# Attention, gated convolution and expert layer on one core: the first two batches in one written order of single steps, part of the low halves on GpSimd

## The chip, the core and the metric

The kernel runs on one core of a Trainium2 chip. The metric is device time in microseconds (us) of one execution. Engines are named as the profile names them: PE (TensorE matmul) with PEld (its weight load), DVE (VectorE), ACT (ScalarE), POOL (GpSimd) and SP (SyncE, which issues the DMAs).

## The reference

For each of 8 batches, 8 heads of width 64 and 576 positions, a linear attention, an RMS norm, a gated value layer with a 5-tap convolution, and a second, larger layer. The expert weights arrive as float64, which the device takes as pairs of 32-bit words.

```python
kv  = einsum('bhsd,bhse->bhde', k, v)                 # per head, 64 x 64
out = einsum('bhsd,bhde->bhse', q, kv)
x   = out / sqrt(mean(out*out, -1) + 1e-6) * g_norm   # heads side by side: 576 x 512
gate = sigmoid(sum_k conv_w[k] * x_padded[k:k+576])   # 5 taps along the positions
x   = (gate * (x @ w_val)) @ w_out                    # 512 x 512 each; "y" below
# then the second layer: w_in (512 x 1024), gelu, norm, w_sg over positions, w_out, residual
```

## The kernel before

A batch's 576 positions are five tiles of 128 (the last one overlaps and brings 64 new ones). Everything that a matmul reads is kept as a high part, rounded to the format that TensorE takes at full speed, and a low part, the difference to the full value; a product of two split operands is three matmuls per slice of 128 (`gemm3`, L228: high by high, low by high, high by low), 12 matmuls for one 128x512 tile.

One batch goes through these steps. `kv` (L280) multiplies K and V of all tiles, and ACT copies the eight 64x64 blocks into a block-diagonal tile `kvbd` (L288, L289). `o` (L296) multiplies q of one tile by it. ACT squares (L302), DVE sums over the head (`reduce`, L305), the mean is taken on DVE for batch 0 and on GpSimd for the others (L306), GpSimd raises it to -0.5 (`pow`, L307), and DVE multiplies the tile by it (`scale`, L310). PE turns the tile round (`xT`, L325), ACT writes its high part (`Xh`, L329) and its full value (`X`, L330), and DVE the low part from PSUM (`Xl`, L334). The convolution is one tap on ACT (L353) and four on DVE for each of four column groups (`taps`, L359), the sigmoid is ACT's (L362). `val` is the product with w_val (L228), DVE multiplies it by the gate (`gated`, L387), ACT makes its high part (L388), and DVE or GpSimd its low part (`z low`, L391; GpSimd for two of four from batch 1 on). `y` is the product with w_out, copied by ACT (L405) and stored (L407).

The two weights w_val and w_out are split on the chip in four pieces each. A piece is one ACT step (L131), TENSOR_SCALAR steps on DVE (L141, L142, L143), two SCALAR_TENSOR_TENSOR steps on DVE (L134, L138), a high part on ACT (L178), and then the low part. For all of w_val and the first piece of w_out, the low part is the sum of three PE matmuls (label `l`, L196) copied by ACT (L197); for the other pieces of w_out it is a subtraction (L186) and an addition (L188) on DVE.

The order is partly written out: all of batch 0 up to its `z low` parts stands under a manual schedule, in which each engine gets its instructions in program order. Then a loop over batches and eight steps per batch (four `val`, four `y`) puts one product of the current batch, one or two `o` tiles of the next, and the deferred work of earlier steps (a list with due slots, `later`) one behind the other. Every PE result takes one of eight PSUM banks (`bank`, L89), in order of request. `busy(n)` puts n matmuls without use on PE. After the last batch a second phase follows, with products hv, hu, sg and out on PE to the end.

Loads go through one queue on SP, in program order; a load whose buffer is not free holds up all behind it.

Of the kernel before, what the change touches and what calls it, by code (L numbers as in the profile page):

```python
# [13 lines left out]
I32 = mybir.dt.int32  # L14
# [51 lines left out]
def body(ctx, tc, qT, k, v, gcol, w_val, conv_w, w_out, w_in, g_ln, w_sgT, b_sg, w_out2, out, out_r):  # L66
# [45 lines left out]
    nc.gpsimd.memset(mhalf, -0.5)  # L112
    kvbd = [sb(f"kvbd{i}", [NK, P]) for i in range(2)]
# [31 lines left out]
    def split(src, h, l, raw=None, tmp=None, k=None, last=nc.gpsimd.tensor_tensor):  # L145
# [20 lines left out]
        def first():  # L166
            if wide:
                st["steps"] = wide_parts(st["raw"].rearrange("p (n t) -> p n t", t=2),
                                         sb("cv", [3, n]) if tmp is None else tmp)
                st["steps"][0]()  # L170

        def steps():

            ops = st["steps"][1]
            yield ops[0]()
            yield ops[1]()
            a = ops[2]()
            act(h, flat(a), AF.Copy)  # L178
            yield
            yield ops[3]()  # L180
            c = ops[4]() if last else ops[4](l, flat)
            yield
            if last is None:
                st["parts"] = a, c
                return
            last(flat(a), flat(a), f32(h), op=ALU.subtract)  # L186
            yield
            tt(l, flat(a), flat(c), op=ALU.add)  # L188
            yield

        def summed():

            a, c = st["parts"]
            ps = bank("l", n)
            for i, (w, x) in enumerate(((ident, flat(a)), (signed[:, 1], h), (signed[:, 0], c))):
                nc.tensor.matmul(flat(ps), lhsT=w, rhs=x, start=(i == 0), stop=(i == 2))  # L196
            return lambda: act(l, flat(ps), AF.Copy)  # L197

        def rest():
            r = st["raw"]  # L200
            if wide:
                for _ in steps():
                    pass
# [8 lines left out]
        return load, work, first, steps if wide else lambda: iter([rest()]), summed if wide and last is None else lambda: lambda: None  # L212
# [32 lines left out]

    class Attention:
        def __init__(self, b):
            self.b = b
            self.xh, self.xl = (sb(f"X{b % 2}{i}", [NK, MAIN], F32R) for i in "hl")

        def load_kv(self):
            b = self.b
            self.k, self.v = sb("K", [5, D]), sb("V", [5, D])
            for c in (((0, 2), (2, 4)) if b == 0 else ((0, 4),)):
                for t_, src in ((self.k, k), (self.v, v)):
                    dma(t_[:, c[0]:c[1], :], src[b, P * c[0]:P * c[1], :].rearrange("(c p) d -> p c d", p=P))
            dma(self.k[:, 4, :], k[b, TOK[4]:, :])
            dma(self.v[REST:, 4, :], v[b, MAIN:, :])
            nc.gpsimd.memset(self.v[:REST, 4, :], 0.0)

        def load_q(self):
            self.q = sb("Q", [NK, S])
            dma(self.q, qT[self.b].rearrange("m p s -> p m s"))

        def kv(self, half):
            if half == 0:
                if self.b:
                    pk = bank("kv")
# [13 lines left out]
            if half:  # L282
                later(0, self.kv_out, 0)

        def kv_out(self):
            bd = kvbd[self.b % 2]
            for pk, j in self.pk3:
                act(bd[:DH, j, :DH], pk[:DH, :, :DH], AF.Copy)  # L288
                act(bd[DH:, j, DH:], pk[DH:, :, DH:], AF.Copy)  # L289

        def o(self, t, wait=3):
            bd = kvbd[self.b % 2]
            o = TOK[t]
            po = bank("o")
            for j in range(NK):
                nc.tensor.matmul(po[:, j * P:(j + 1) * P], lhsT=self.q[:, j, o:o + P], rhs=bd[:, j, :], start=True, stop=True)  # L296
            st = sb("st", [3, 8], bufs=5)
            xo = tmp(D)
            x3 = xo.rearrange("p (h d) -> p h d", d=DH)

            def square():
                act(xo, po, AF.Square)  # L302

            def norm(small=nc.gpsimd.tensor_scalar):
                nc.vector.tensor_reduce(st[:, 0], x3, axis=AX.X, op=ALU.add)  # L305
                small(st[:, 1], st[:, 0], 1.0 / DH, 1e-6, op0=ALU.mult, op1=ALU.add)  # L306
                nc.gpsimd.tensor_tensor(st[:, 2], st[:, 1], mhalf, op=ALU.pow)  # L307

            def scale():
                tt(x3, po.rearrange("p (h d) -> p h d", d=DH),  # L310
                   st[:, 2].unsqueeze(2).to_broadcast([P, 8, DH]), op=ALU.mult)

            if wait is None:
                square()
                return norm, scale, lambda: self.transpose(t, xo, True)
            later(0, square, 0)
            later(0, norm, 0)
            later(wait - 1, scale, 0)
            later(wait, lambda: self.transpose(t, xo), 0)

        def transpose(self, t, xo, apart=False):
            o, n = (TOK[t], P) if t < 4 else (MAIN, REST)
            pt = bank("xT")
            for j in range(NK):
                nc.tensor.transpose(pt[:, j * P:(j + 1) * P], xo[:, j * P:(j + 1) * P], ident)  # L325
# [659 lines left out]
```

## Time and profile before

| | |
|---|---|
| time, median of 3 runs | 728.8 us (728.15 to 728.98) |
| profiled execution | 727.04 us |
| its span in the trace | 725.2 us, so 1.84 us lie around the span |
| PE busy | 709.9 us (98% of the span) |
| DVE, ACT, POOL busy | 583.6, 350.3, 152.5 us (80%, 48%, 21%) |
[...]
| y of batch 1 begins on PE | at 93.15 us |

Rows of the timeline hold the start, the duration, the engine, the line, the operation, the tile written and the tile read with their shapes, and the number of instructions in a run; square brackets give the idle time of that engine before the row and what ended it. Where a run has several instructions, its duration from the first start to the last end says less than the distance of their starts, which is what the prediction counts with ("pitch"): 7.38 us for ten taps is a pitch of 0.74.

### The profile page before, as it was taken

The numbers are of one execution on the slowest core, as the hardware profiler recorded it, in microseconds if no ns is written. First come the engines' busy times: TensorE is split into PE (matmuls) and PEld (weight loads), VectorE is DVE, ScalarE is ACT, GpSimd is POOL, SyncE is SP. The second block draws the span as 40 slices with busy tenths as digits, with TensorE's granted clock in tenths as the row PEclk, the third lists the DMA queues.
The fourth block names the chain that finished last, engine by engine and source line by source line (L and its number), as shares of the span: only waits on it lengthen the run. The fifth ranks groups of instructions, "written<-read, shape, count | busy, mean of one in ns | idle before, by whom it ended". The sixth has DMA issues, their size and how long they took to land.

```text
span 725.2 us, 11759 instructions
## 1 busy us (share of the span) xinstructions
PE 709.9 (98%) x4490; PEld 620.7 (86%) x4490; DVE 583.6 (80%) x1127; ACT 350.3 (48%) x667; POOL 152.5 (21%) x173
## 2 busy tenths in 40 slices
PE   8997999999999999999999999999999999999998
PEld 7785888879888888899889889898899898898897
DVE  6699979999989999699976866867856857867662
ACT  4667465676566674475433433424333424334230
POOL 1414437262727361112000000000100000100000
PEclk9999999999999999999999999999999999999999
DMA  9945253525462213433220321122241122111202
GB/s 338 331 141 201 96 195 119 217 80 207 130 251 84 88 30 125 158 120 103 73 81 36 103 89 30 58 88 74 78 156 30 58 88 74 58 59 45 102 1 87
DMA packets 56712, 81.19 MB, mean 112 GB/s; under 512 B 3665, under 2 KB 29265, under 8 KB 55633
## 3 DMA queue, kind: packets, MB, share of 16 engines
q1 hardware_dynamic: 56656, 80.45, 32.2%
q8 instruction: 35, 0.57, 0.3%
q14 instruction: 21, 0.16, 0.1%
HBM read 61.56 MB, written 18.87 MB: 111 GB/s over the span
## 4 chain that ended last, share of the span: by engine, by line
PE 58%; DVE 1%; DMA 0%; ACT 0%; POOL 0%; issue 0%; POOLq 0%; SPq 0%; DVEq 0%
PE sg L587 16%; PE hv L478 14%; PE out L228 14%; PE hu L228 12%; PE hur L228 2%; PE y L228 1%; PE val L228 1%; DMA raw<-y_main 0%; DVE Z L391 0%; DVE T L387 0%; POOL cv L186 0%; DVE cv L134 0%; DVE V L188 0%; DVE cv L141 0%; ACT X1h L455 0%
## 5 line engine op out<-in xcount | busy, mean ns | idle before, releaser
L359 DVE SCALAR_TENSOR_TENSOR G<-X,cw,G 128x576 f32<-128x576 f32 x128 | 98.3, 819 | 5.2 <-ACT G L353 5.1
L228 PE MATMUL y<-Z,WOh 128*128 128x512 f32 (+1 forms) x320 | 96.8, 376 | 0.0
L490 POOL TENSOR_TENSOR bmv<-bmv,mhalf 128x1 f32<-128x1 f32 x36 | 21.4, 596 | 342.6 <-DVE bmv L489 342.6
L478 PE MATMUL hv<-wiv,X1h 128*128 128x512 f32 x256 | 83.1, 390 | 0.1
L228 PE MATMUL out<-Z,K 128*128 128x512 f32 x256 | 83.0, 389 | 0.0
L228 PE MATMUL hu<-X1h,wiu 128*128 128x512 f32 x256 | 79.2, 391 | 0.0
L307 POOL TENSOR_TENSOR st<-st,mhalf 128x8 f32<-128x8 f32 x40 | 70.2, 1762 | 7.0 <-DVE st L306 4.7
L228 PEld LDWEIGHTS y<-Z,WOh 128*128 128x128 f32 x320 | 57.9, 188 | 9.6
L467 ACT ACTIVATE T<-T 128x512 f32<-128x512 f32 x68 | 42.9, 631 | 44.7 <-DVE T L464 44.7
L228 PE MATMUL y<-Z,WOl 128*128 128x512 f32 (+1 forms) x160 | 57.9, 369 | 0.0
L228 PEld LDWEIGHTS out<-Z,K 128*128 128x128 f32 x256 | 48.1, 188 | 10.0
L478 PEld LDWEIGHTS hv<-wiv,X1h 128*128 128x128 f32 x256 | 47.8, 188 | 10.0 <-ACT X1h L455 0.5
L588 DVE SCALAR_TENSOR_TENSOR T<-sg,gln,WOl 128x288 f32<-128x288 f32 x64 | 32.7, 515 | 26.3 <-PE sg L587 26.2
L228 PEld LDWEIGHTS hu<-X1h,wiu 128*128 128x128 f32 x256 | 46.6, 188 | 8.3
L228 PE MATMUL hu<-X1l,wiu 128*128 128x512 f32 x128 | 50.0, 390 | 0.0
L478 PE MATMUL hv<-wiv,X1l 128*128 128x512 f32 x128 | 49.9, 390 | 0.0
L228 PE MATMUL out<-Z,V 128*128 128x512 f32 x128 | 49.8, 389 | 0.0
L599 ACT ACTIVATE Z<-T 128x512 fp32r<-128x512 f32 x32 | 20.1, 630 | 57.5 <-DVE T L598 57.5
L296 PEld LDWEIGHTS o<-kvbd,Q 128*128 128x128 f32 x320 | 40.3, 191 | 2.5 <-issue 0.3
L296 PE MATMUL o<-kvbd,Q 128*128 128x128 f32 x320 | 40.7, 275 | 0.1
L228 PE MATMUL val<-X0h,WV 128*128 128x512 f32 x128 | 40.7, 399 | 0.0
L228 PE MATMUL val<-X1h,WV 128*128 128x512 f32 x128 | 40.6, 398 | 0.0
(174 smaller groups left out, 1699.4 us busy)
## 6 DMA issues: line engine op xcount, KB each, us to landing
Q<-in_qT_dram SPq DMA_DIRECT2D x8, 1152.0 KB, 5.4
y_main<-Y SPq DMA_DIRECT2D x8, 1024.0 KB, 3.8
raw<-y_main SPq DMA_DIRECT2D x32, 256.0 KB, 3.1
Y<-y_main SPq DMA_DIRECT2D x32, 256.0 KB, 4.1
out_dram<-Y SPq DMA_DIRECT2D x32, 256.0 KB, 2.3
K<-in_k_dram SPq DMA_DIRECT2D x7, 1024.0 KB, 5.6
V<-in_v_dram SPq DMA_DIRECT2D x7, 1024.0 KB, 8.5
raw<-in_w_in_dram SPq DMA_DIRECT2D x16, 256.0 KB, 4.7
```

The source lines that it names most:

```text
L228: nc.tensor.matmul(ps, lhsT=a[:, kt, msl], rhs=x[:, kt], start=(i == 0), stop=(i == 3 * NK - 1))
L296: nc.tensor.matmul(po[:, j * P:(j + 1) * P], lhsT=self.q[:, j, o:o + P], rhs=bd[:, j, :], start=True, stop=True)
L307: nc.gpsimd.tensor_tensor(st[:, 2], st[:, 1], mhalf, op=ALU.pow)
L359: stt(gate[:, m], x32[:, m, j:j + S], cw3[:, m, j:j + 1], gate[:, m], op0=ALU.mult, op1=ALU.add)
L467: act(w, w, AF.Tanh, scale=CG * AG)
L478: nc.tensor.matmul(ps, lhsT=a[:, kt], rhs=p2["wiv"][:, w, kt], start=(i == 0), stop=(i == 3 * NK - 1))
L490: nc.gpsimd.tensor_tensor(mv[:, 3:4], mv[:, 2:3], mhalf[:, 0:1], op=ALU.pow)
L587: nc.tensor.matmul(ps, lhsT=a[:, msl], rhs=w, start=(n == 0), stop=(n == len(mm) - 1))
L588: later(0, lambda: stt(vs[:, sl], ps, gln_s[:, m:m + 1], p2["bsg"][:, sl], op0=ALU.mult, op1=ALU.add))
L599: act(g[:, 0], x, AF.Copy)
```

## The change

A table ORDER, a string of 356 words, now says one by one in which order the steps of batches 0 and 1 go, and those of batch 2 up to its transposes. A word is one step: `La0` loads piece 0 of w_val, `a2h` is the high part of its piece 2, `b0s` the subtraction and `b0+` the addition in the low part of piece 0 of w_out; `o`, `q`, `r`, `m`, `w`, `s`, `t` are product, square, reduce, mean, pow, scale and transposes of an attention tile (`s24`: batch 2, tile 4), `h`, `x`, `l` the high part, the full value and the low part of x, `p` a tap, `S` a sigmoid, `v`, `z`, `Z`, `u` the val product, gated, z high and z low, `y`, `Y` the product and its copy. A star puts the step on GpSimd; `~n` puts n matmuls without use into the PSUM bank of the step. The table runs under the manual schedule, then the loop goes on at batch 1, step 4.

What differs in content:

- K and V of batch 0 are loaded behind two pieces of w_val, not behind all four and a piece of w_out; q of batch 0 comes in two halves; w_val's other two pieces and w_out come behind them.
- The low parts of w_val pieces 2 and 3 and of all four pieces of w_out are a subtraction and an addition on GpSimd (twelve instructions of 128x512). Only pieces 0 and 1 of w_val keep the three matmuls.
- x low: 4 of 4 tiles of batch 0, 3 of 4 of batch 1 and 4 of 4 of batch 2 are a subtraction on GpSimd that reads the full value and the high part from SBUF (before: DVE, from PSUM).
- z low: 3 of 4 of batch 0 and 3 of 4 of batch 1 on GpSimd (before: none and 2).
- Most means of batches 0 to 2 are taken on ACT. Batch 0's eight kvbd copies are shared out between ACT and DVE.
- Matmuls without use: 30 at the start as before, and 15 more in all.
- K, V and q of batch 3 are asked for right behind the table; the gates of batch 2 are due at steps 4 and 5 of batch 1.

SP, from the program's start. `wiu` and `Y` are the buffers into which pieces of w_val and w_out are loaded. Before:

```order
L164 DMA wiu_91<-in_w_val_dram 128x4x256 x4
L164 DMA Y_93<-in_w_out_dram 128x4x256
L256 DMA K_106<-in_k_dram 128x2x512
L256 DMA V_107<-in_v_dram 128x2x512
L256 DMA K_106<-in_k_dram 128x2x512
L256 DMA V_107<-in_v_dram 128x2x512
L257 DMA K_106<-in_k_dram 128x512
L258 DMA V_107<-in_v_dram 64x512
L688 DMA raw_115<-in_conv_w_dram 128x40
L263 DMA Q_117<-in_qT_dram 128x4x576
```

After:

```order
L183 DMA wiu_93<-in_w_val_dram 128x4x256 x2
L308 DMA K_137<-in_k_dram 128x2x512
L308 DMA V_138<-in_v_dram 128x2x512
L308 DMA K_137<-in_k_dram 128x2x512
L308 DMA V_138<-in_v_dram 128x2x512
L311 DMA K_137<-in_k_dram 128x512
L313 DMA V_138<-in_v_dram 64x512
L320 DMA Q_146<-in_qT_dram 128x4x256
L320 DMA Q_146<-in_qT_dram 128x4x320
L828 DMA gcol_81<-in_gcol_dram 128x1
L829 DMA gln_82<-in_g_ln_dram 128x4
L183 DMA wiu_93<-in_w_val_dram 128x4x256 x2
```

Three loads of 512 KB have moved from ahead of K to behind q.

DVE, from the last scale of batch 0 on. `G` is the gate, `cw` the taps' weights, `wiv`, `Z`, `cv` temporaries of the weights' split. Before:

```order
L310 TENSOR_TENSOR T_323<-o_317,st_322 128x512
L334 SCALAR_TENSOR_TENSOR X0l_96<-xT_369,gcol_79,X0h_95 128x4x128
L334 SCALAR_TENSOR_TENSOR X0l_96<-xT_382,gcol_79,X0h_95 128x4x128
L359 SCALAR_TENSOR_TENSOR G_86<-X_12_85,cw_81,G_86 128x576 x6
L349 TENSOR_TENSOR XR_614<-X_12_85,XR_614 128x4x64
L359 SCALAR_TENSOR_TENSOR G_86<-X_12_85,cw_81,G_86 128x576 x10
```

After:

```order
L383 TENSOR_TENSOR T_283<-o_239,st_282 128x512
L153 SCALAR_TENSOR_TENSOR wiv_94<-wiv_94 128x512
L157 SCALAR_TENSOR_TENSOR Z_96<-wiu_93,Z_96 128x512
L162 TENSOR_SCALAR wiv_94<-wiv_94 128x512
L157 SCALAR_TENSOR_TENSOR Z_96<-wiu_93,Z_96 128x512
L801 TENSOR_TENSOR cw_83<-cv_102 128x20
L157 SCALAR_TENSOR_TENSOR wiv_94<-Y_95,wiv_94 128x512
L160 TENSOR_SCALAR wiv_94<-Y_95 128x512
L453 SCALAR_TENSOR_TENSOR G_88<-X_13_87,cw_83,G_88 128x576 x5
L161 TENSOR_SCALAR wiv_94<-wiv_94 128x512
L453 SCALAR_TENSOR_TENSOR G_88<-X_13_87,cw_83,G_88 128x576 x3
L153 SCALAR_TENSOR_TENSOR wiv_94<-wiv_94 128x512
```

The low parts of x have left DVE, and weight steps that stood ahead of batch 0's norm now stand ahead of its taps and between them.

POOL, from the last pow of batch 0 on (`st` holds the norm's small values). Before:

```order
L307 TENSOR_TENSOR st_322<-st_322,mhalf_73 128x8
L259 MEMSET V_551 64x512
L306 TENSOR_SCALAR st_562<-st_562 128x8
L307 TENSOR_TENSOR st_562<-st_562,mhalf_73 128x8
L306 TENSOR_SCALAR st_569<-st_569 128x8
```

After:

```order
L379 TENSOR_TENSOR st_282<-st_282,mhalf_73 128x8
L408 TENSOR_TENSOR X0l_98<-X_13_87,X0h_97 128x4x128 x4
L242 TENSOR_TENSOR wiv_94<-wiv_94,WOh_85 128x512
L242 TENSOR_TENSOR Z_96<-Z_96,WV_84 128x512
L244 TENSOR_TENSOR WOl_86<-wiv_94 128x4x128
L242 TENSOR_TENSOR Z_96<-Z_96,WV_84 128x512
L314 MEMSET V_491 64x512
L244 TENSOR_TENSOR WV_84<-Z_96 128x4x128
L379 TENSOR_TENSOR st_485<-st_485,mhalf_73 128x8
L379 TENSOR_TENSOR st_497<-st_497,mhalf_73 128x8
```

Where POOL had one memset between the pows of batch 0 and those of batch 1, it now has nine subtractions and additions of 128x512 as well.

The core of the diff (a line with only "..." marks what is left out):

```diff
+ORDER = """
+W30 La0 La1 LK0a LV0a LK0b LV0b LK0c LV0c Lq0a Lq0b Lg La2 La3 Lb0 Lcw a00 a1a a10 a0a a11 kv0a a01 a12 a13 a02 kv0b
...
+a34 x02 b03 a24 h02 c5 x04 b0h b04 p010 p000 b10 kv1 Lq1 k1b k1a l00* Lb3 p011 p020 b1a p001 l02* p012 p002 p013 b11
...
+"""
...
+            elif step == "s":
+                nc.gpsimd.tensor_tensor(st["a"], st["a"], f32(h), op=ALU.subtract)
+            else:
+                last(l, st["a"], st["c"], op=ALU.add)
...
+    def own(ps):
+        for i in range(idle[0]):
+            nc.tensor.matmul(ps[:, :P], lhsT=ident, rhs=ident, start=True, stop=True)
+        idle[0] = 0
+        return ps
...
+        def mean(self, t, by=None):
+            st = self.tile[t]["st"]
+            if by is act:
+                act(st[:, 1], st[:, 0], AF.Identity, scale=1.0 / DH, bias=eps)
+            else:
+                nc.gpsimd.tensor_scalar(st[:, 1], st[:, 0], 1.0 / DH, 1e-6, op0=ALU.mult, op1=ALU.add)
...
+        def low(self, t, by=None):
+            xh, xl = (x[:, :, TOK[t]:TOK[t] + P] for x in (self.xh, self.xl))
+            if by is None:
+                stt(xl, self.tile[t]["pt"], gcol_s, f32(xh), op0=ALU.mult, op1=ALU.subtract)
+            else:
+                nc.gpsimd.tensor_tensor(xl, self.at(t), f32(xh), op=ALU.subtract)
...
-    wv_pieces = first_weight((wv[:, 0], wv[:, 1]), w_val, [first[0][:, i] for i in range(4)], tmps, [None] * 4)
+    wv_pieces = first_weight((wv[:, 0], wv[:, 1]), w_val, [first[0][:, i] for i in range(4)], tmps, [None, None, pool_tt, pool_tt])
     wo_pieces = first_weight(wo, w_out, [spare[:, 0], spare[:, 1], first[0][:, 0], first[0][:, 1]],
-                             tmps[:2] * 2, [None, tt, tt, tt])
+                             tmps[:2] * 2, [pool_tt, pool_tt, pool_tt, pool_tt])
...
     with tc.manual_schedule():
...
+        for op in ORDER.split():
+            op, n = (op + "~0").split("~")[:2]
+            idle[0] = int(n)
+            if op[0] == "L":
+                load(op[1:])
+            elif op[0] == "W":
+                busy(int(op[1:]))
+            elif op in ("kv0a", "kv0b"):
+                atts[0].kv("ab".index(op[3]), False)
+            else:
+                act_part(op.rstrip("*"), op[-1] == "*")
+    marks = [latest()] * 4
+    atts.append(Attention(3))
+    atts[3].load_kv()
+    atts[3].load_q()
...
-    for b in range(B):
-        if b:
-            moe = Moe(atts[b].xh, atts[b].xl, gate, y_main[b])
+    for b in range(1, B):
+        moe = moes[b] if b == 1 else Moe(atts[b].xh, atts[b].xl, gate, y_main[b])
...
-        for s in range(8):
+        if b == 1:
+            whole = unbroken(lambda: (nn.kv(0), nn.kv(1)))
+        for s in range(4 if b == 1 else 0, 8):
...
-            if nxt and s in (5, 7):
-                later(0, lambda a=nxt, m=s - 5: a.gates((m, m + 1)), 2)
+            if nxt and s in ((4, 5) if b == 1 else (5, 7)):
+                later(0, lambda a=nxt, m=2 * (s > 4) if b == 1 else s - 5: a.gates((m, m + 1)), 2)
```

## Rows read from the trace of the kernel before

**Rows 1.** The page: busy time, share of the span and instructions, each engine.

```profile
PE 709.9 (98%) x4490; PEld 620.7 (86%) x4490; DVE 583.6 (80%) x1127; ACT 350.3 (48%) x667; POOL 152.5 (21%) x173
```

**Rows 2.** PE's waits over the whole span: total us, times, longest us.

```profile
PE xT L325 <- DVE T L310: 5.9, 7, 2.9
PE warm L244 <- POOL X L234: 2.3, 1, 2.3
```

**Rows 3.** The same view, from 0 to 100 us alone.

```profile
PE xT L325 <- DVE T L310: 3.4, 3, 2.9
```

**Rows 4.** Busy time per engine, 27.7 to 93.2 us: PE, PEld, DVE, ACT, POOL, clock.

```profile
27.70:93.20 65.50, 59.55 (x533) 50.40 (x533) 62.18 (x101) 42.37 (x78) 25.39 (x25) 1.00 0.48 170
```

**Rows 5.** ACT's timeline: first and last of w_val's four pieces, first kvbd copy.

```profile
4.54 0.68 ACT L131 ACTIVATE wiv<-wiu 128x512 f32<-128x512 f32 x1 [2.32 <-DMA wiu<-in_w_val_dram]
...
8.64 0.69 ACT L131 ACTIVATE Z<-wiu 128x512 f32<-128x512 f32 x1 [0.73 <-DMA wiu<-in_w_val_dram]
...
17.94 0.22 ACT L288 ACTIVATE kvbd<-kv 64x64 f32<-64x64 f32 x1 [1.28 <-PE kv L280]
```

**Rows 6.** PE's timeline: attention of batch 0, and around batch 1's first y.

```profile
16.56 1.62 PE L280 MATMUL kv<-V,K 128*64 128x64 f32 x48
...
20.70 4.70 PE L296 MATMUL o<-kvbd,Q 128*128 128x128 f32 x40
...
90.25 2.55 PE L280 MATMUL kv<-V,K 128*64 128x64 f32 x80
...
93.15 0.48 PE L228 MATMUL y<-Z,WOh 128*128 128x512 f32 x1
...
95.07 0.60 PE L325 MATMUL xT<-ident,T 128*128 128x128 f32 x4
95.42 0.48 PE L228 MATMUL y<-Z,WOh 128*128 128x512 f32 x1
```

**Rows 7.** POOL's timeline: the five pows of batch 0.

```profile
23.47 8.09 POOL L307 TENSOR_TENSOR st<-st,mhalf 128x8 f32<-128x8 f32 x5 [4.65 <-DVE st L306]
```

**Rows 8.** DVE's timeline: weight steps, a scale, taps, reduces.

```profile
6.94 1.28 DVE L134 SCALAR_TENSOR_TENSOR wiv<-wiv 128x512 int32<-128x512 int32 x2
8.14 0.75 DVE L143 TENSOR_SCALAR wiv<-wiv 128x512 int32<-128x512 int32 x2
...
31.86 0.68 DVE L310 TENSOR_TENSOR T<-o,st 128x512 f32<-128x512 f32 x1
...
39.79 7.38 DVE L359 SCALAR_TENSOR_TENSOR G<-X,cw,G 128x576 f32<-128x576 f32 x10
...
53.15 2.46 DVE L305 TENSOR_REDUCE st<-T 128x8 f32<-128x512 f32 x4
```

**Rows 9.** POOL's timeline: four of its fourteen z low subtractions, first and last among them.

```profile
89.85 1.28 POOL L391 TENSOR_TENSOR Z<-T,Z 128x512 fp32r<-128x512 f32 x1
...
115.67 1.30 POOL L391 TENSOR_TENSOR Z<-T,Z 128x512 fp32r<-128x512 f32 x1 [1.17 <-ACT Z L388]
...
188.42 1.29 POOL L391 TENSOR_TENSOR Z<-T,Z 128x512 fp32r<-128x512 f32 x1
...
286.95 1.35 POOL L391 TENSOR_TENSOR Z<-T,Z 128x512 fp32r<-128x512 f32 x1 [2.30 <-ACT Z L388]
```

**Rows 10.** DVE's timeline: instructions beside a row of Rows 9, and the same without.

```profile
90.43 0.69 DVE L387 TENSOR_TENSOR T<-val,G 128x512 f32<-128x512 f32 x1 [0.16 <-ACT X L330]
...
116.16 0.95 DVE L143 TENSOR_SCALAR cv<-cv 128x256 int32<-128x256 int32 x1
...
128.17 0.28 DVE L143 TENSOR_SCALAR cv<-cv 128x256 int32<-128x256 int32 x1
...
129.72 0.42 DVE L188 TENSOR_TENSOR wiv<-cv 128x256 fp32r<-128x256 f32 x1
...
188.45 1.54 DVE L188 TENSOR_TENSOR wiv<-cv 128x256 fp32r<-128x256 f32 x1
...
287.67 0.78 DVE L141 TENSOR_SCALAR cv<-raw 128x256 int32<-128x256 int32 x1
```

More of the change, by code (lines that the diff above doesn't have):

```diff
@@ L201, in rest @@
             if wide:
-                for _ in steps():
-                    pass
+                steps()
             else:
@@ L304, in norm @@
[L304 to L315, printed above, removed]
@@ new lines, in o, with transpose @@
+        def o(self, t, wait=3):
+            self.product(t)
+            later(0, lambda: self.square(t), 0)
+            later(0, lambda: self.sums(t), 0)
+            later(0, lambda: self.mean(t), 0)
+            later(0, lambda: self.root(t), 0)
+            later(wait - 1, lambda: self.scale(t), 0)
+            later(wait, lambda: self.transpose(t), 0)
+        def transpose(self, t):
+            self.turn(t)
+            if t < 4:
+                self.high(t)
+            self.full(t)
+            if t < 4:
+                self.low(t)
@@ new lines, in val, with out_product, done @@
+        def val(self, m):
+            self.product(m)
+            later(0, lambda: (self.gated(m), self.high(m)), 0)
+            later(0, lambda: self.low(m, m in (0, 2)), 0)
+        def out_product(self, m):
+            self.ps[m] = own(bank("y", self.n))
+            gemm3(self.ps[m], wo, m, self.z[:, 0], self.z[:, 1])
+        def done(self, m):
+            if self.y is None:
+                self.y = sb("Y", [NK, self.n])
+            act(self.y[:, m], self.ps[m], AF.Copy)
+            self.left -= 1
+            if not self.left:
+                dma(self.dst, self.y)
@@ L627, in latest, with product @@
         return list(found.values())
-    def product():
-        return next(i for i in reversed(nc.cur_bb.bb.instructions) if i.engine == mybir.EngineType.PE)
+    def product(engine=mybir.EngineType.PE):
+        return next(i for i in reversed(nc.cur_bb.bb.instructions) if i.engine == engine)
     def unbroken(fn):
@@ new lines, in act_part @@
+    def act_part(op, other):
+        kind = op[0]
+        if kind in "ab":
+            return (wv_pieces if kind == "a" else wo_pieces)[int(op[1])][3](op[2])
+        if kind == "c":
+            return cw_step(op[1:])
+        b = int(op[2] if op[:2] == "kv" else op[1])
+        a = atts[b]
+        if op[:2] == "kv":
+            a.kv(0, False)
+            a.kv(1, False)
+        elif kind == "k":
+            a.kv_out((int(op[2]) if b == 0 else 0, "ab".index(op[-1])), nc.vector if b == 0 and op[-1] == "b" else act)
+        elif kind in "oqrwst":
+            {"o": a.product, "q": a.square, "r": a.sums, "w": a.root, "s": a.scale, "t": a.turn}[kind](int(op[2]))
+        elif kind == "m":
+            a.mean(int(op[2]), None if other else act)
+        elif kind == "h":
+            if b == 2 and not hasattr(a, "xh"):
+                a.operands()
+            a.high(int(op[2]))
+        elif kind == "x":
+            a.full(int(op[2]))
+        elif kind == "l":
+            a.low(int(op[2]), pool_tt if other else None)
+        elif kind == "p":
+            a.tap(int(op[2]), int(op[3])) if op[3] != "0" else a.taps(int(op[2]))
+        elif kind == "S":
+            a.sigmoid(int(op[2]))
+        elif kind == "g":
+            {"X": a.rest_high, "L": a.rest_low, "r": a.rest_gate}[op[2]]()
+        else:
+            moe = moes[b] = moes.get(b) or Moe(a.xh, a.xl, gate, y_main[b])
+            m = int(op[2])
+            if kind == "u":
+                moe.low(m, other)
+            else:
+                {"v": moe.product, "z": moe.gated, "Z": moe.high, "y": moe.out_product, "Y": moe.done}[kind](m)
```

385 lines of the change are left out of this document (188 added, 197 removed).

## The prediction

> **What bounds the kernel now.** I read the page first: PE is busy for 709.9 of 725.2 us [rows 1], so the end moves by what PE idles, or does for nothing, and by little else. The waits of PE say where it idles: most of it is transposes that wait for DVE's scale, 5.9 us in seven waits [rows 2], of which 3.4 us lie before 100 us [rows 3], in the stretch that the change rewrites. After that PE nearly always has work, and everything behind keeps its distance to it. So I look for one point at which the old and the new order can be laid beside each other: the first y matmul of batch 1, at 93.15 us. There kv of batch 3 is done (90.25 to 92.8) and two of batch 2's transposes are still to come, a pitch of 0.35 each from 95.07 to 95.42 [rows 6]; with these two counted in, the point is 93.9. In the new order the written table ends in front of that matmul with all five transposes done, and kv of batch 3 follows. The question is when DVE, which scales before PE can transpose, lets PE come to this point. From 27.7 to 93.2 DVE is busy for 62.18 of 65.50 us [rows 4]: beside PE it is the engine without room, idle for 3.3 us.
>
> The sum goes against the profiled execution (727.04 us, of which 1.84 lie around the span). The median of the runs is 1.76 above it, so I add the difference to the median.
>
> **Part 1, K and V earlier.** The four pieces of w_val land 1.37 us apart, (8.64 - 4.54) / 3 [rows 5]. With two of them ahead, K and V of batch 0 (2.36 MB, 4.5 times a piece) land by 5.9 + 6.2 = 12.1. Half of kv is done by then, and the rest ends at about 13.4, where it now ends at 18.2 (16.56 + 1.62) [rows 6]. The copies to kvbd, eight on one engine from 17.94 at about 0.23 [rows 5], become four on each of two, so o begins at 14.7 and not at 20.70 [rows 6]: 6.0 earlier.
>
> **Part 2, the norm of batch 0.** The first pow comes 2.8 us after the first o now (23.47 and 20.70) [rows 6, 7]; with the mean on ACT I add 0.2 and get 17.7. Five pows of 8.09 in all end at 25.8. But DVE has to do, between its kvbd copies (14.4) and the last scale: ten reduces and scales at a pitch of 0.6 (2.46 for four at 53.15, one scale 0.68), four SCALAR_TENSOR_TENSOR steps of the weights at 0.6, nine TENSOR_SCALARs at 0.34 and five small ones at 0.2 [rows 8], 12.5 us, and about 0.8 of waits for pow. The last scale ends at 27.7, where it now ends at 32.5 (31.86 + 0.68) [rows 8]. Some 5 us are won here, and PE can take val 5.6 us earlier with the transposes between. The PE work saved (three pieces' low parts) lies where PE waits anyway, and counts nothing. The fifteen matmuls without use lie there too.
>
> **Part 3, DVE from 27.7 to batch 2's last scale.** By the order of the changed kernel there are 32 taps at a pitch of 0.74 (23.7), ten SCALAR_TENSOR_TENSOR steps at 0.6 (6.0), ten TENSOR_SCALARs and two small subtractions at 0.34 (4.1), one z low (0.6) and cw (0.2): 34.6 us in instructions that read two operands from SBUF, or are TENSOR_SCALARs. Then 28 that are neither, reduces, scales, gated products and one x low from PSUM, at 0.6 (16.8) [rows 8]. All 51.4 us bring DVE to 79.1, and with the 3 us of waits that it has now [rows 4] to 82; transposes 0.5 and kv 2.5 [rows 6] put y of batch 1 at 85.0. If nothing else happened, that would be 8.9 us earlier than 93.9.
>
> **Part 4, what GpSimd's new work costs DVE.** This decides. GpSimd's z low has the shape and form of the new subtractions and additions, and takes 1.28 to 1.35 us [rows 9]. Beside it DVE's instructions come out long if they read two operands from SBUF or are TENSOR_SCALARs: the one at 116.16 takes 0.95 where its like takes 0.28, that at 287.67 0.78, and the one at 188.45, which begins 0.03 us after GpSimd's, takes 1.54 where its like takes 0.42 [rows 9, 10]. Each ends only behind the end of GpSimd's instruction: DVE stands, 1.12 us of 1.29 in the third case. The gated product at 90.43, one operand of which comes from PSUM, takes the usual 0.69 in the middle of GpSimd's [rows 9, 10]. Over the fourteen z lows DVE loses 7.2 us, 0.51 each (three of them nothing, six 0.65 to 0.70, one 1.12).
>
> [...]
>
> Before the point there are now 25 such instructions on GpSimd: twelve of the weights, seven x lows, six z lows, some 32 us of it, beside DVE's 51.4, two thirds of which can be held up. From below: as long as DVE works at one of its 28 other instructions (16.8 us), GpSimd runs free; even if all that time lay beside GpSimd's, 32 - 16.8 leaves 15 us that meet, less what DVE would have idled, 11 to 12 of it lost. From a plain count: 25 x 0.51 = 12.8. From above: 25 x 1.12 = 28. That DVE loses nothing needs GpSimd's 25 to fall into its waits, of which there are 3 us. I take 0.68, the commonest single loss, for each: 17.0, because here most of DVE's neighbours are taps and weight steps, where in the fourteen cases many were scales and gated products.
>
> DVE then ends at 79.1 + 17.0 = 96.1; its 3 us of waits vanish in that, since what it waits for is ready by then. Transposes and kv add 3.0: y of batch 1 at 99.1, against 93.9, 5.2 us late. PE stands for it, its val products waiting for banks and for transposes that hang on DVE's scale.
>
> **Part 5, given back.** After this point DVE is about 6 us further on against PE than before, since batch 2's norm is all done. The waits for scale past 100 us (5.9 - 3.4 = 2.5 in four) [rows 2, 3] can shrink; most hang on PE's own order, so I take 1.0 back, of a possible 2.5 and at least nothing. The loads of batch 3 and the store of batch 0's y change places on SP; nothing waits for them within 10 us of their landing, so they count nothing; if the store came so late that its buffer held up the next y copy, it would be some tenths. Sum: 5.2 - 1.0 = +4.2, rounded to 4.1 for the profiled execution, 731.1, and 732.9 against the median.
>
> **Rivals.** First, the collisions cost little: GpSimd's instructions fall beside PSUM readers and waits. For it: the order is written step by step, so it can put them there; three of fourteen did so by chance. Against it: 32 us of GpSimd and only 16.8 + 3 us of room. With nothing lost y comes at 85.0, 8.9 early, 719.9; with half of the plain count (6.4) lost, 726.3. Second, the loss is the old mean, 12.8: DVE at 91.9, y at 94.9, 1.0 late, and 1.0 given back: 728.8, no change. The case that the order does not do what it says, because the waits between engines bring PE back to the old pace, ends here too. [...] The forecast is itself on the slower side, its turning point is 12 to 13 us lost (79.1 + 3.0 + 12 = 94.1): above that, PE waits longer in the end than it won at the start.
>
> **How the numbers follow.** This kernel's measurement can tell about 0.2% (1.5 us) from no change. Forecast, 730.3 to 738: 0.5. Collisions mostly covered, 719.9 to 727.3: 0.2, all faster. Old mean, within 1.5 us of 728.8: 0.2. More than 738: 0.1. Faster 0.2, same 0.2, slower 0.6. The range leaves out the 0.1 at the top and about a third of the first rival's 0.2 at the bottom: 721 to 738.5. The forecast's own range is 730.3 to 738.
>
> **What would show it.** First o on PE near 14.7 and last scale of batch 0 near 27.7 for parts 1 and 2. In the stretch from there to batch 1's y, DVE's taps beside GpSimd's subtractions with 1.1 to 1.6 us where 0.8 is usual, and DVE busy throughout for parts 3 and 4; a mean tap of 0.75 to 0.8 would say that the loss is small and the first rival holds. [...] The prediction falls if GpSimd waits for DVE in these encounters and not DVE for GpSimd, or if PE's order ahead of that point does not hang on DVE's scale.

## The result, and the profile after

The changed kernel takes 737.4 us (median of four runs, 736.44 to 738.52) against 728.9 us of the kernel before, run beside it: ratio 1.0114, interval 1.0092 to 1.0136. It is 8.5 us slower; the forecast was 4.1 us slower. Its profiled execution is the slowest of its four runs, 738.52 us with a span of 736.7.

The page first (busy time, share of the span, instructions), which answers to [rows 1], and the waits of PE (total us, times, longest us), which answer to [rows 2]:

```profile
PE 713.2 (97%) x4466; PEld 622.8 (85%) x4466; DVE 589.9 (80%) x1105; ACT 348.6 (47%) x672; POOL 193.1 (26%) x194
```

```profile
PE xT L390 <- DVE T L383: 8.5, 8, 3.3
PE val L266 <- DVE T L484: 3.7, 1, 3.7
...
PE y L266 <- POOL WOl L244: 1.4, 1, 1.4
PE kv L337 <- DMA V<-in_v_dram: 1.1, 2, 0.7
```

PE idles for 23.5 us of the span and not for 15.3, about half of it for DVE's scale (L383) and a gated product (L484), both DVE's. GpSimd's busy time has grown by 41 us, DVE's has not shrunk: 589.9 after, 583.6 before.

Where the forecast's landmarks came, on PE's timeline, first o, batch 0's last transposes, and batch 1's first y behind kv (to be laid beside [rows 6]):

```profile
16.02 1.16 PE L358 MATMUL o<-kvbd,Q 128*128 128x128 f32 x8 [0.27 <-ACT kvbd L349]
...
32.11 0.66 PE L390 MATMUL xT<-ident,T 128*128 128x128 f32 x4 [2.26 <-DVE T L383]
...
103.37 2.55 PE L337 MATMUL kv<-V,K 128*64 128x64 f32 x80
105.85 0.50 PE L266 MATMUL y<-Z,WOh 128*128 128x512 f32 x1
```

First o at 16.0 (forecast 14.7), the last scale of batch 0 done at 32.1 (27.7), batch 1's first y at 105.9 (99.1), which is 12.0 late against the 93.9 of the kernel before.

Busy time per engine from 32.1 to 102.7 us (PE, PEld, DVE, ACT, POOL, granted clock of PE), the row that answers to [rows 4]: DVE works for 68.44 of 70.60 us, GpSimd for 55.25.

```profile
32.10:102.70 70.60, 60.23 (x424) 49.53 (x424) 68.44 (x85) 34.96 (x69) 55.25 (x38) 0.90 0.37 127
```

DVE's and GpSimd's timelines at two places show what DVE does in that time:

```profile
28.78 1.50 DVE L162 TENSOR_SCALAR Z<-Z 128x512 int32<-128x512 int32 x1
30.20 1.25 DVE L157 SCALAR_TENSOR_TENSOR cv<-raw,cv 128x20 f32<-128x20 uint32 x1
31.38 0.68 DVE L383 TENSOR_TENSOR T<-o,st 128x512 f32<-128x512 f32 x1
...
65.53 4.85 DVE L160 TENSOR_SCALAR wiv<-wiu 128x512 int32<-128x512 int32 x2
```

```profile
28.72 5.63 POOL L408 TENSOR_TENSOR X0l<-X,X0h 128x512 fp32r<-128x512 f32 x4
...
65.71 0.70 POOL L314 MEMSET V<- 64x512 f32 x1
66.39 2.48 POOL L493 TENSOR_TENSOR Z<-T,Z 128x512 fp32r<-128x512 f32 x2
68.84 1.25 POOL L408 TENSOR_TENSOR X1l<-X,X1h 128x512 fp32r<-128x512 f32 x1
```

A TENSOR_SCALAR that needs 0.42 takes 1.50, a step on 20 columns that needs 0.18 takes 1.25, each beside one of batch 0's four x lows; and two TENSOR_SCALARs that need 0.75 together take 4.85, until GpSimd is through with a memset, two z lows and an x low in a row. A memset alone holds up a TENSOR_SCALAR too, 0.76 for 0.42 (DVE, then GpSimd):

```profile
24.89 0.76 DVE L161 TENSOR_SCALAR Z<-Z 128x512 f32<-128x512 f32 x1
```

```profile
24.85 0.52 POOL L314 MEMSET V<- 64x512 f32 x1
```

The taps tell it in one line each. By line, engine and tile, from 30 us to batch 1's first y: count, busy us, mean ns of one. Before:

```profile
L359 DVE SCALAR_TENSOR_TENSOR G<-X,cw,G 128x576 f32<-128x576 f32 x32 | 24.1, 811 | 0.5 <-ACT G L353 0.5
```

After:

```profile
L453 DVE SCALAR_TENSOR_TENSOR G<-X,cw,G 128x576 f32<-128x576 f32 x32 | 33.2, 1075 | 0.1
```

The same 32 taps take 9.1 us more. Over all of DVE up to that point, 20 instructions take over 0.12 us more than is usual for their kind, 19.6 us together: 2.5 of it (at 24.89, 28.78 and 30.20) ahead of batch 0's last scale, 16.5 from there to batch 2's last scale, and 0.6 on a z low behind that.

### The profile page after: what moved, and what is told of

Same layout as the page of the kernel before. It is cut to its first block, busy times and chain, and to the rows that moved or that the text cites. A ratio compares the mean times of both kernels' runs of the same rounds, so it can differ in the third digit from the quotient of the medians.

```text
span 736.7 us, 11709 instructions
## 1 busy us (share of the span) xinstructions
PE 713.2 (97%) x4466; PEld 622.8 (85%) x4466; DVE 589.9 (80%) x1105; ACT 348.6 (47%) x672; POOL 193.1 (26%) x194
## 4 chain that ended last, share of the span: by engine, by line
PE 57%; DMA 1%; DVE 1%; ACT 0%; POOL 0%; issue 0%; POOLq 0%; SPq 0%; DVEq 0%
PE sg L692 16%; PE out L266 13%; PE hv L583 13%; PE hu L266 12%; PE hur L266 2%; DMA raw<-y_main 1%; PE y L266 1%; PE val L266 0%; DVE Z L493 0%; DVE T L484 0%; ACT X1h L560 0%; POOL cv L201 0%; DVE V L202 0%; DVE cv L153 0%; DVE cv L160 0%
## 5 line engine op out<-in xcount | busy, mean ns | idle before, releaser
L453 DVE SCALAR_TENSOR_TENSOR G<-X,cw,G 128x576 f32<-128x576 f32 x128 | 108.2, 891 | 8.4 <-ACT G L450 8.3
L379 POOL TENSOR_TENSOR st<-st,mhalf 128x8 f32<-128x8 f32 x40 | 73.1, 1838 | 22.9 <-ACT st L373 20.9
L266 PE MATMUL val<-X0h,WV 128*128 128x512 f32 x128 | 43.5, 419 | 4.6 <-DVE T L484 3.7
```

Source lines behind the costliest of these rows:

```text
L266: nc.tensor.matmul(ps, lhsT=a[:, kt, msl], rhs=x[:, kt], start=(i == 0), stop=(i == 3 * NK - 1))
L453: stt(gate[:, m], x32[:, m, j:j + S], cw3[:, m, j:j + 1], gate[:, m], op0=ALU.mult, op1=ALU.add)
```

## The experiments

Theory A is the prediction's: a 128x512 subtraction or addition on GpSimd holds DVE up, and DVE's end sets PE's pace. B is that the work taken off DVE does help and something else is at fault; C puts it on PE's clock; D, E and F concern the load order. All times are medians of four to twelve runs, ratios are against runs of the kernel before made beside them.

**Everything back on DVE (e1_all_dve), and one kind each (e2, e3, e4).** In e1:

```diff
-                nc.gpsimd.tensor_tensor(st["a"], st["a"], f32(h), op=ALU.subtract)
+                tt(st["a"], st["a"], f32(h), op=ALU.subtract)
...
-    ... w_val, ..., [None, None, pool_tt, pool_tt])
+    ... w_val, ..., [None, None, tt, tt])
-                             tmps[:2] * 2, [pool_tt, pool_tt, pool_tt, pool_tt])
+                             tmps[:2] * 2, [tt, tt, tt, tt])
...
-                nc.gpsimd.tensor_tensor(xl, self.at(t), f32(xh), op=ALU.subtract)
+                tt(xl, self.at(t), f32(xh), op=ALU.subtract)
...
-                moe.low(m, other)
+                moe.low(m, False)
```

e2 has the first three of these edits, e3 the fourth, e4 the fifth.

> The changed kernel with all 29 starred or weight subtractions and additions of 128x512 (12 of the weights, 11 x lows, 6 z lows) done by DVE at the same places of the table, from the same tiles. Theory A (GpSimd's instruction holds DVE up): the 25 of them ahead of batch 1's first y cost DVE about 19.4 us of standing in the trace of after, 0.78 each; on DVE they cost 25 x 0.6 = 15. So the first y of batch 1 comes 4 to 5 us earlier than 105.85, near 101.5, no tap takes over 0.95 us, and the time is 733 (731 to 735). Theory B (the offload does relieve DVE; the loss is made by the written order and the late start): DVE gets 15 us more work, the first y comes near 120, the time is 748 to 752. Theory C (the loss is PE's fall to the lower clock in its gaps): gaps as before or longer, 737 or more.

> The changed kernel with only the twelve weight instructions on DVE. In the trace of after, about 9.4 us of DVE's standing lie beside these twelve; on DVE they take 12 x 0.6 = 7.2. Theory A: 2 us earlier, and PE's waits for GpSimd's weight parts (1.4 and 0.8) gone: 735 (733.5 to 736.5). Theory B: 7 us more work for DVE, 744 to 745.

> The changed kernel with only the eleven starred x lows (seven ahead of batch 1's first y) on DVE. Beside the seven, DVE stands for about 5.4 to 8 us in the trace of after, according to how the 4.1 us at 65.9 are shared out between an x low, two z lows and a memset; on DVE they cost 4.2. Theory A: 1 to 4 us earlier, 733.5 to 736.5. Theory B: 4 us later, 741 to 742.

> The changed kernel with only the six z lows of the table on DVE. Beside them DVE stands for about 3 to 5 us in the trace of after; on DVE they cost 3.6. Theory A: between 1.5 us earlier and no change, 736 to 737.5. Theory B: 3.6 us later, 741.

| | time | ratio (interval) | batch 1's first y |
|---|---|---|---|
| changed kernel | 737.4 | 1.0114 (1.0092 to 1.0136) | 105.85 |
| e1, all on DVE | 733.6 | 1.0074 (1.0057 to 1.0091) | 100.30 |
| e2, weights on DVE | 734.3 | 1.0089 (1.0071 to 1.0106) | 102.03 |
| e3, x lows on DVE | 735.5 | 1.0106 (1.0089 to 1.0122) | 104.27 |
| e4, z lows on DVE | 736.3 | 1.0113 (1.0095 to 1.0131) | 103.58 |

DVE gets 15 us more to do and the kernel becomes faster. B asked for 748. e1's interval lies just under that of the changed kernel (1.0091 and 1.0092); e2 to e4 by themselves are within the uncertainty, but all have their first y earlier, as A said. In e1 the taps are at their old pace (same view and window as above):

```profile
L453 DVE SCALAR_TENSOR_TENSOR G<-X,cw,G 128x576 f32<-128x576 f32 x32 | 25.2, 810 | 0.1
```

**Six fewer on GpSimd, none more on DVE (e5_l_path); the same and the rest on DVE (e6_l_path_dve).** In the table, the steps `s` and `+` of three pieces become `l` (three PE matmuls) and `c` (an ACT copy):

```diff
-    ... w_val, ..., [None, None, pool_tt, pool_tt])
+    ... w_val, ..., [None, None, None, None])
-                             tmps[:2] * 2, [pool_tt, pool_tt, pool_tt, pool_tt])
+                             tmps[:2] * 2, [None, pool_tt, pool_tt, pool_tt])
```

> The changed kernel, but the low parts of w_val pieces 2 and 3 and of w_out piece 0 come again from three PE matmuls and an ACT copy, at the same places of the table: six GpSimd instructions less, and nothing for DVE instead. Theory A (GpSimd's instruction holds DVE up, and DVE's end sets batch 1's first y): six times about 0.78 us less on DVE, 4.7 us; first y near 101, time 733 (732 to 735), though PE gets 4 us more. Theory B (offloading to GpSimd is good, PE is the bound): 4 us later, 741.

> The same three pieces through PE and ACT, and all other starred or weight steps of the table on DVE as in e1_all_dve: no 128x512 subtraction or addition is left on GpSimd in the table. Against e1_all_dve DVE loses six instructions at 0.6, 3.6 us. If DVE's end sets the time, first y 3.6 us earlier than 100.3, 96.7, and the time 730 (729 to 731.5), still not under the kernel before, since DVE stands idle from 9.3 to 14.3 us in the new load order. If what is left over the kernel before in e1_all_dve is of another kind (the written order's PE work or clock), no gain or a loss: 733.5 or more.

e5 takes 733.5 us (1.0082, 1.0069 to 1.0094), first y at 101.96: as A said, PE's 4 us more notwithstanding (its interval still touches that of the changed kernel, by 0.0002). e6 missed: 733.8 us (1.0075, 1.0062 to 1.0088), first y at 101.95, no better than e1. Its DVE now waits, for ACT's squares and once for nothing that the profile names:

```profile
44.98 0.69 DVE L369 TENSOR_REDUCE st<-T 128x8 f32<-128x512 f32 x1 [2.45 <-ACT T L365]
...
60.98 0.69 DVE L485 TENSOR_TENSOR T<-val,G 128x512 f32<-128x512 f32 x1 [1.95 <-issue]
```

So with the collisions gone, DVE's list alone no longer sets the pace in this order.

e5 also has the longest stand of all, one TENSOR_SCALAR beside four x lows without a gap between them (DVE, then GpSimd):

```profile
28.96 5.48 DVE L161 TENSOR_SCALAR wiv<-Y 128x512 int32<-128x512 int32 x1
```

```profile
29.24 4.92 POOL L409 TENSOR_TENSOR X0l<-X,X0h 128x512 fp32r<-128x512 f32 x4
```

**The clash by itself (e7_extra_tt, e8_extra_memset).** The kernel before, with GpSimd work that nothing reads, beside batch 0's taps (`scr` is a tile of its own):

```diff
         z += [moe.val(m, True) for m in (2, 3)]
+        for i in range(12):
+            nc.gpsimd.tensor_tensor(scr[:, 1], scr[:, 1], scr[:, 0], op=ALU.subtract)
         for a in (0, 2):
```

and in e8 `for i in range(30): nc.gpsimd.memset(scr[:, 1], 0.0)` at the same place.

> The kernel before, with twelve subtractions of 128x512 on GpSimd that read and write a tile which nothing else uses; they begin behind batch 0's last pow, near 31.6 us, some nine of them beside batch 0's sixteen taps on DVE. Nothing waits for them but GpSimd itself. Theory A: nine taps stand for about 1.0 each, the gated products of batch 0 come 9 us later, the time is 736 (734.5 to 738). Rival (they share no resource, what holds DVE in the changed kernel is its order): as the kernel before, 727 to 729.

> The kernel before, with thirty memsets of 128x512 on GpSimd at the same place, on a tile that nothing else uses: about the same 15.6 us of GpSimd time, but they only write. Theory A, if it is the reading of two operands that clashes: taps keep their 0.74, the time is that of the kernel before (727 to 729). If any work of GpSimd holds a tap up, as in e7_extra_tt: 734 or more.

e7 takes 737.9 us (1.0140, 1.0126 to 1.0153): twelve subtractions, 9.9 us, 0.82 each. e8 takes 728.4 us (1.0002, 0.9992 to 1.0012): no loss. The taps of e7 from 36 to 54 us, then those of e8 from 36 to 48 us, by line:

```profile
L361 DVE SCALAR_TENSOR_TENSOR G<-X,cw,G 128x576 f32<-128x576 f32 x11 | 16.9, 1602 | 0.5 <-ACT G L355 0.5
```

```profile
L361 DVE SCALAR_TENSOR_TENSOR G<-X,cw,G 128x576 f32<-128x576 f32 x16 | 11.8, 808 | 0.5 <-ACT G L355 0.5
```

GpSimd's rows beside them, subtractions in e7 and memsets in e8:

```profile
35.40 11.85 POOL L770 TENSOR_TENSOR scr<-scr 128x512 f32<-128x512 f32 x7
```

```profile
32.65 11.61 POOL L770 MEMSET scr<- 128x512 f32 x20
```

A tap beside a subtraction takes double (1602 ns), beside a memset no longer than without either (808; 811 in the kernel before). (No TENSOR_SCALAR stood beside these thirty memsets, so e8 says nothing of that form.) GpSimd pays too: seven subtractions take 11.85 us here, 1.7 each, where one alone takes 1.28 [rows 9].

**PE's clock (e11_fill).** In the table, `t04~5` becomes `t04~15` and `t14` becomes `t14~15`.

> The changed kernel with 10 and 15 more matmuls without use ahead of batch 0's last transposes and of the transposes at 71 us, where PE waits 2.3 and 3.3 us for DVE's scale and the granted clock falls to 0.83. Theory A (DVE sets the pace, PE's clock matters little): 0 to 1 us gained, 736.5 to 737.5. Theory C (the clock makes the part of the loss that the collisions don't explain): 3 us or more gained, under 734.5.

737.3 us (1.0141, 1.0110 to 1.0172), as the changed kernel. Windows of the changed kernel, then of e11 (last but two columns the granted clock):

```profile
30.00:40.00 10.00, 7.89 (x101) 7.08 (x102) 10.00 (x11) 4.90 (x10) 8.97 (x6) 0.83 0.54 190
...
70.00:80.00 10.00, 8.97 (x43) 8.09 (x44) 9.33 (x18) 7.75 (x16) 4.05 (x3) 0.83 0.65 230
```

```profile
30.00:40.00 10.00, 8.75 (x120) 7.48 (x119) 10.00 (x11) 4.87 (x10) 8.97 (x7) 1.00 0.76 253
...
70.00:80.00 10.00, 10.00 (x60) 8.79 (x59) 10.00 (x17) 8.09 (x16) 6.07 (x6) 1.00 0.70 236
```

The clock did fall for part of these windows: it is 0.50 from 34 to 36 and from 72 to 74 us, each time behind a wait of PE for DVE (2.3 and 3.3 us), where the kernel before has 1.00 from 27.7 to 93.2 [rows 4]. Kept at 1.00 in both windows, it gave nothing back (e11 has a dip to 0.83 at 90 to 100 us, where the changed kernel has 1.00). A third dip, at 50 to 60 us (0.70 in the changed kernel, 0.67 in e11), is left: PE waits there 3.7 us, in both, for the gated product that frees a PSUM bank, so there is no bank to put matmuls into. C falls for the two places that were tried.

**The load order (e10_kv_first, e9_more_first, then e12 with two, three and four pieces ahead, e13_w_first).** All but e13 are the kernel before with another order at the start.

> The kernel before, with the change's load order alone: K, V and q of batch 0 behind two pieces of w_val, the other two and w_out 0 behind them, and their split on DVE behind batch 0's scales. First o near 15 us instead of 20.7. Theory E (what the prediction counted for parts 1 and 2): 4 to 5 us gained, 723 to 725. Theory D: DVE idles 5 us more ahead of 15 us and less behind, the three pieces' steps (7 us) now stand ahead of the taps, no gain: 728 to 730.

> The kernel before, with one more weight piece (w_out 1) loaded ahead of K and V and split on DVE while it waits for them: the opposite of the change's load order. DVE stands idle for 5.2 us between 15 and 30 us in the trace of before; the piece's seven steps, 3.4 us, go there, K and V come 1.4 us later. Theory D (up to batch 1's first y DVE's work plus its idle time set the pace, so that early idle time is what matters): 2 us gained, 726 (725 to 727). Theory E (the sooner o begins the better, as the change's load order has it): 1.4 us lost, 729.5 to 730.

e10 takes 731.1 us (1.0040), but its first o comes at 19.7 and not near 15, since the low parts of w_val still stand ahead of kv on PE. e9 takes 730.5 us (1.0036), worse than either theory said; its edit put 13 matmuls without use ahead of kv's second half and the first reduce comes 3.1 us later, not 1.4. Neither decides anything. e12 has PE do kv and o first:

```diff
-        for copy in [p[4]() for p in wv_pieces[:2]]:
-            copy()
-        busy(3)
         att.kv(0)
...
         att.kv(1)
         slots.drain()
...
         steps = [att.o(t, None) for t in range(5)]
+        for copy in [p[4]() for p in wv_pieces[:n]]:
+            copy()
...
+        in_turn(*wv_pieces[n:])
+        in_turn(wo_pieces[0])
```

where n pieces of w_val are loaded ahead of K and V, and the others and w_out 0 are split behind batch 0's norm.

> The kernel before, with K and V behind two pieces of w_val as in the change, and with PE doing both halves of kv and the five o ahead of the low parts of w_val (in e10_kv_first these still stood ahead of kv, so that the first o came only 1 us earlier). Pieces 2 and 3 and w_out 0 are split on DVE behind batch 0's norm. First o near 15.5 us, batch 0's scales some 4.5 us earlier than in e10_kv_first. Theory E (an early K and V is worth what it brings the first o forward): 4 us under e10_kv_first's 731, 726.5 to 727.5, a little faster than the kernel before. Theory F (DVE idle from 10 to 16 us, and the weight steps then stand ahead of the taps: nothing is won): 729 to 731.

> The same with three pieces of w_val ahead of K and V: first o 1.4 us later than with two, 2.2 us of DVE's weight steps in the time before K and V land instead of ahead of the taps. Theory F: 0.8 us better than with two pieces. Theory E: 1.4 us worse.

> The same with all four pieces of w_val ahead of K and V, only w_out 0 behind them. Theory F: another 0.8 us better than with three; near the kernel before, 727 to 729. Theory E: another 1.4 us worse.

The first o on PE with two, and with four pieces:

```profile
16.82 4.70 PE L296 MATMUL o<-kvbd,Q 128*128 128x128 f32 x40 [0.88 <-ACT kvbd L289]
```

```profile
20.02 4.70 PE L296 MATMUL o<-kvbd,Q 128*128 128x128 f32 x40 [1.47 <-DMA Q<-in_qT_dram]
```

The times are 731.3, 731.4 and 732.0 us (1.0043, 1.0046, 1.0053, intervals some 0.0014 either way). First o 3.2 us earlier gives 0.6 us at most, so E is out; F's step of 0.8 per piece the other way isn't there either. With two pieces DVE stands idle until the first reduce, and what it could have done by then comes later, ahead of the taps (5.1 us later than in the kernel before, where they begin at 35.07):

```profile
18.61 0.69 DVE L305 TENSOR_REDUCE st<-T 128x8 f32<-128x512 f32 x1 [8.01 <-ACT T L302]
...
40.13 11.75 DVE L359 SCALAR_TENSOR_TENSOR G<-X,cw,G 128x576 f32<-128x576 f32 x16
```

With four pieces it stands idle nearly as long, 7.4 us, and then once more, for transposes that stand on PE behind the low parts of all four pieces, so that the taps begin at 41.13:

```profile
32.67 0.75 DVE L334 SCALAR_TENSOR_TENSOR X0l<-xT,gcol,X0h 128x512 fp32r<-128x512 f32 x1 [4.26 <-PE xT L325]
```

So the three differ in more than the first o, and F was not tested cleanly; E, by which four pieces lose 2.8 us to two, fails even so. All three are some 3 us slower than the kernel before. They share w_val's low parts behind o and w_out 0 behind the norm; which of the two costs it was not tried.

> e1_all_dve (the changed kernel with all its 128x512 subtractions and additions on DVE), with all four pieces of w_val ahead of K and V again, and the first five DVE steps of pieces 2 and 3 ahead of batch 0's attention, in the time when DVE waits for K and V. In e1_all_dve PE waits 3.2 us for an x low and 2.4 us for w_val's low part, both of which stand behind these weight steps on DVE. Theory F (what is left of the loss once GpSimd is out of it comes from weight steps that the new load order pushed behind batch 0's attention): 2 to 4 us under e1_all_dve, 729.5 to 731.5. Theory E: 2 to 3 us over it, 736.

e13 takes 734.4 us (1.0084, 1.0066 to 1.0103): nothing won over e1. The last two steps of w_val's pieces kept their late places in the table, and PE waits for them for 4.0 us instead of 2.4.

**Relief for DVE in the kernel before (e14_less_dve, e14_l_wo1).** The second of the two edits, which e14_l_wo1 has alone:

```diff
-                             tmps[:2] * 2, [None, tt, tt, tt])
+                             tmps[:2] * 2, [None, None, tt, tt])
...
+            if b == 0 and s == 4:
+                later(0, lambda: wo_pieces[1][4]()(), 0)
```

> The kernel before, with two reliefs of DVE that put nothing on GpSimd: batch 0's five means on ACT (as in the change), and the low part of w_out piece 1 from three PE matmuls and an ACT copy instead of two DVE steps, placed ahead of batch 0's second y, where PE waits 2.9 us for DVE's scale. DVE's end sets that wait: 0.85 + 1.2 us less on DVE, so up to 2 us gained, 726 to 727. If ACT's mean costs as much as it saves (each goes over to ACT and back) and PE's 1.3 us of matmuls come on top: 728 to 729.

> The kernel before with the second relief alone (w_out piece 1's low part through PE and ACT): 1.2 us gained if DVE's end sets the wait at 64.6 us, 727; nothing or 1 us lost if PE's own order does.

e14_l_wo1 takes 726.3 us (0.9973, 0.9964 to 0.9983): faster than both kernels. Its PE waits 1.5 us ahead of the second y of batch 0 where the kernel before waits 2.9 [rows 2], and the three matmuls begin right there (the first of them, with an f32 operand, is two in the trace, 0.46 us for the pair, where one of y, with rounded operands, takes 0.23 from start to start):

```profile
64.43 0.66 PE L325 MATMUL xT<-ident,T 128*128 128x128 f32 x4 [1.54 <-DVE T L310]
64.92 1.02 PE L196 MATMUL l<-wiv,ident 128*128 128x512 f32 x2
```

But this fills a wait and saves none: batch 1's first y comes at 94.28, and at 94.36 in e8, whose first o is as late (21.91 in both). The gain appears later, in transposes at 147 us, where PE's wait for DVE's scale all but goes (the kernel before, then e14_l_wo1); from 125 to 156 us PE idles for 0.5 us instead of 1.6:

```profile
147.25 0.63 PE L325 MATMUL xT<-ident,T 128*128 128x128 f32 x4 [1.30 <-DVE T L310]
```

```profile
146.92 0.63 PE L325 MATMUL xT<-ident,T 128*128 128x128 f32 x4 [0.17 <-DVE T L310]
```

With the means on ACT as well it is 732.4 us (1.0053, 1.0037 to 1.0069), 6 us more than e14_l_wo1: ACT takes the first mean only behind all five squares, and DVE waits for the pow that follows (ACT, then DVE):

```profile
27.12 0.60 ACT L304 ACTIVATE T<-o 128x512 f32<-128x512 f32 x1 [0.30 <-PE o L298]
27.61 0.67 ACT L741 ACTIVATE st<-st,eps 128x8 f32<-128x8 f32 x3
```

```profile
29.69 0.69 DVE L312 TENSOR_TENSOR T<-o,st 128x512 f32<-128x512 f32 x1 [3.04 <-POOL st L309]
```

The first scale comes 7.3 us behind the first o (22.38) instead of 4.5; where the rest of the 6 us arises was not traced. In the changed kernel the means stand between the squares, and DVE does not wait for the first pow (done at 21.2, first scale at 22.41).

## Why the prediction was half right

The side and the mechanism were right, the size was not: 4.1 us forecast, 8.5 measured. The steps that failed are the end of part 2, the last scale of batch 0 (27.7 forecast, 32.1 measured), and the waits of DVE that were to vanish behind it (nothing forecast, 2.2 us measured); together they are 6.6 of the 6.8 us by which batch 1's first y misses its forecast. The sum of DVE's work and collisions between the two last scales came out. By its own steps:

**What bounds the kernel, part 3.** Right. DVE is busy for 68.44 of 70.60 us up to batch 2's last scale; forecast were 51.4 of work and 17.0 of collisions, 68.4. e1, which has no collisions and 25 instructions at 0.6 (15 us) more on DVE, seems to confirm the plain sum, 100.30 for 85.0 + 15. That agreement is in part luck: batch 0's last scale ends there at 29.6, not at 27.7, and DVE idles for 0.7 us behind it, not for 3.0.

**Parts 1 and 2: mis-sized by 4.4 us.** The last scale of batch 0 was put at 27.7 and ended at 32.1. The kvbd copies end 1.5 us late, at 15.9 (first o 16.0 for 14.7; PE waits 1.1 us for V, which landed later than the sum of megabytes said). Then 2.5 us are collisions, where the prediction had none: two with x lows that were already running ahead of that scale (28.78 and 30.20, 2.2 us), and the TENSOR_SCALAR beside a memset (24.89, 0.3 us). DVE idles 1.3 us and not 0.8, mostly for a piece of w_val that lands only at 19.26. And the premise that an earlier o is worth having got no support: the first o is 4.7 us earlier than in the kernel before, batch 0's last scale 0.5 us, and in e12 3.2 us of it are worth 0.6 at most.

**Part 4, the collisions: right in kind; the sum came out by two errors that cancel.** From the trace the 25 cost 19.6 us, 0.78 each against 0.68 forecast; e7, by time alone, has 0.82. But three of them, the first two x lows and the last z low, lie outside the stretch in which the prediction counted all 25, and in the stretch 16.5 us were lost against 17.0. What was not foreseen is that a TENSOR_SCALAR can stand behind several GpSimd instructions in a row: 4.1 us at 65.9 where one collision was counted. The upper bound of 1.12 each held. Of the signs that would bring the prediction down, GpSimd waiting for DVE is there too: the 25 were put at some 32 us of GpSimd's time and take 38.7, 1.55 each where 1.28 is usual [rows 9]. At 36.91 (1.84 us) it waits beside DVE's standing; at 76.05 (2.64) and 95.35 (1.72) it waits in its place, with every DVE instruction there at its usual length.

**"The 3 us of waits vanish": wrong.** DVE still idles for 2.2 us between 32.1 and 102.7. With 4.4 and 2.2, and 0.1 more from batch 2's last scale to the y (3.1 for 3.0), the first y is 6.7 us later than forecast; it came 6.8 later, at 105.85.

**Part 5, given back.** 12.0 us late at the first y, 11.5 us longer span: 0.5 was given back, not 1.0. This is within what single executions scatter: from the first y to the end it takes 630.9 us in the changed kernel and 629.7 to 631.2 in e1 to e6. (The sum of 4.2 was also written down as 4.1.)

**From the profiled executions to the medians.** The span grew by 11.5 us, the median by 8.5. The profiled execution of before lay 1.8 us under its median, that of after lies 1.2 over its own. The 3 us between them are scatter of single executions, and the prediction carried only the first 1.8 of it. Against the profiled executions, on which the sum was made, the miss is larger than it looks, 11.5 for 4.1.

**The rivals.** Both (collisions covered, or at the old mean) are out by e1, e5 and e7. For the 0.1 given to more than 738 no run shows a cause of its own: 16.5 us were lost beside GpSimd in that stretch, less than the 17.0 counted, and the y is late because batch 0's norm was. PE's clock did fall, to 0.50 in three places, and cost nothing that could be measured in the two where e11 kept it at 1.00.

**What stays open.** Without any collision, e1 is still slower than the kernel before by a ratio of 1.0074. Up to batch 1's first y PE idles for 14.4 us in e1, 17.3 in the changed kernel and 8.8 in the kernel before. In e1 it waits for an x low (3.2), for w_val's low part (2.4) and for w_out's (1.5); of these three, the kernel before has only the x low, 0.6:

```profile
PE val L266 <- DVE X0l L408: 3.2, 1, 3.2
...
PE val L266 <- DVE WV L244: 2.4, 1, 2.4
PE y L266 <- DVE WOl L244: 1.5, 1, 1.5
```

That the weight steps stand too late in the written order is a reading of these rows only; e6 and e13 took some of them away and gained nothing.

## What to carry to other kernels

Before moving elementwise work from DVE to GpSimd, sort DVE's neighbouring instructions by what they read. Here it was 20 of those with two operands from SBUF and of the TENSOR_SCALARs that stood, 0.78 us for each of GpSimd's 25 (0.82 in e7), more than the 0.60 from start to start in which DVE did one itself in e1. Those that read PSUM, and the reduces, kept their length beside one of GpSimd's: in the changed kernel 0.68 for the gated products at 53.70 and 57.65 and for the scale at 90.43, 1.27 for the two reduces at 55.73. Beside a memset a tap kept its 0.81 us (e8), and a TENSOR_SCALAR took 0.76 for 0.42. PE and ACT were the better place for the one low part tried: through three PE matmuls, put where PE was waiting anyway, it cost PE nothing there, took two steps off DVE, and was 0.3% faster than the kernel before. And an earlier start was worth little (0.6 us of 3.2) on an engine that does not set the pace; ask first what the engine that does would be doing meanwhile.

## What the runs showed of the hardware

A SCALAR_TENSOR_TENSOR got in between two GpSimd instructions that follow each other (in e7 taps and subtractions alternate, seven subtractions in 11.85 us beside six taps in 9.86; in the changed kernel the one at 31.98 got in ahead of the fourth x low, which takes 1.74). A TENSOR_SCALAR was seen both ways. Twice it stood through all of them: 5.48 us beside four in e5, 4.85 for two beside a memset and three in the changed kernel, with GpSimd at its full pace of 1.25 us meanwhile. At 28.78 and at 37.52 in the changed kernel it got in behind the first, after 1.50 and 1.52 us, and GpSimd's next took 1.45 and 1.48. What decides between the two was not tried. A hold can outlast one GpSimd instruction: 5.48 us in e5, where each of the four takes 1.23.

A TENSOR_SCALAR stood for a memset as well: 0.76 for 0.42 at 24.89 in the changed kernel, and 0.69 for 0.28 at 126.03 in the kernel before, each beside one of 0.52.
